# Six softmax multiplications moved from GpSimd to VectorE, and the start's small loads moved to other queues, in an attention and MLP kernel

## The chip, the cores and the metric

One Trainium2 chip, one core. The metric is the device time of one execution in microseconds (us). A ratio is the mean time of one kernel's runs over the mean time of the other's runs of the same rounds, so it is not quite the ratio of the medians that are quoted beside it.

Names in the profile: PE is the matrix engine and PEld its weight load; DVE is VectorE; ACT is ScalarE; POOL is GpSimd; SP issues most DMAs. A "q" behind an engine's name (ACTq) marks its instruction queue. L428 is line 428 of the kernel that was profiled. "n = 3" and the like are steps of the kernel's loop over pairs. A "half-clock window" is a stretch, some 3 us long or (after the longest stall) twice that in these traces, in which the granted clock is 0.50 and matrix instructions take about twice as long.

## The reference

```python
# q, k, v: (8, 12, 448, 64) float32; g_q, g_k: (64,); w_in: (768, 2048); w_out: (2048, 768)
def rmsnorm(x, g):
    rms = np.sqrt(np.mean(x * x, axis=-1, keepdims=True) + 1e-06)
    return x / rms * g
q_n, k_n = (rmsnorm(q, g_q), rmsnorm(k, g_k))
scores = scale * np.matmul(q_n, k_n.transpose(0, 1, 3, 2))
attn = np.exp(scores - max)                       # [cut: the maximum is taken off by row]
attn = attn / (np.sum(attn, axis=-1, keepdims=True) + 1e-09)
x = np.matmul(attn, v)                            # [cut: to (8*448, 12*64)]
h = x @ w_in
out = (h * (1.0 / (1.0 + np.exp(-h)))) @ w_out
```

## The kernel before

The kernel takes the heads two by two: 8 batches of 6 pairs, 48 pairs in all. The attention of a batch and the first matrix product of an earlier batch run interleaved, so PE always has something to do once the first batch is through. Only the first batch (pairs 0 to 5) has no product beside it, and there PE waits for the other engines.

The softmax is divided late: the exponentials are weighed with v, and the result x is multiplied by the reciprocal of the sums of the exponentials. The sums are made in two steps: DVE adds the chunks up (L428), then PE multiplies by ones (L444). DVE takes the reciprocal into `r[0]` (L448). For a couple of pairs six small DMAs spread it into `r[0]` and `r[1]`; a single pair (4 and 5 in the first batch) is divided at once.

```python
    def sums(members, width):
        t = ps.tile([P, S], F32, name="tr") if members[0] >= z.NPAIR else bank(S)
        for h in range(2):
            for i, n in enumerate(members):
                nc.tensor.matmul(                                            # L444
                    t[ds(h * D + i * width, width), :], ones[0:R, 0:width], es[n % 2][:, h, :],
                    start=True, stop=True,
                )
        nc.vector.reciprocal(out=r[0], in_=t)                                # L448

    def divide(n, t):
        engine = nc.gpsimd if n < z.NPAIR else nc.vector     # NPAIR is 6: the first batch
        x = xT(*pairs[n])
        engine.tensor_tensor(out=x, in0=x, in1=t, op=ALU.mult)               # L453
        state[n] = None

    def divide_by_sums(n):
        if n > 2 and n % 2 == 1 and not is_single(n - 2):
            for i in range(2):
                divide(n - 3 + i, r[i])              # n = 3: pairs 0, 1; n = 5: pairs 2, 3
        if n > 0 and is_single(n - 1):
            sums([n - 1], D)
            divide(n - 1, r[0])                      # n = 5: pair 4; n = 6: pair 5
        elif n > 0 and n % 2 == 0:
            sums([n - 2, n - 1], D // 2)             # n = 2: pairs 0, 1; n = 4: pairs 2, 3
            ...                                      # [cut: six small DMAs into r[0] and r[1]]
```

Rows are normalised by the same engines in turn: ACT squares, DVE sums the squares, POOL raises them to the power -1/2, and POOL multiplies q by that (for pair 0 DVE does).

```python
def normalise_rows(nc, z, rows, normal, squares, rms, minus_half, engine, together=True):
    for part in ([0, 1],) if together else ([0], [1]):
        for i in part:
            nc.scalar.activation(t, rows[name], AF.Square)                   # L297
            nc.vector.tensor_reduce(out=rms[:, i], in_=t, axis=AX.X, op=ALU.add)   # L298
        nc.vector.tensor_scalar(out=flat, in0=flat, ...)                     # L300
        nc.gpsimd.tensor_tensor(out=flat, in0=flat, in1=half, op=ALU.pow)    # L304
        if 0 in part:
            engine.tensor_tensor(out=by_head, in0=rows["q"], in1=factor, op=ALU.mult)  # L308
```

The start loads the rows of pairs 0 and 1, the gains `g_q` and `g_k` (as columns, for the factor of k), the same gains as rows (for a branch condition), and the first eight pieces of weights, 512 KB each. After the branch the rows of pair 2 are asked for.

```python
    load(state, 0)                                   # rows of pair 0, on SP
    for t, g in ((gq2, g_q), (gk2, g_k)):
        for half in range(2):
            nc.scalar.dma_start(t[ds(half * D, D), :], g.rearrange("(d one) -> d one", one=1))
    load(state, 1)
    for i, g in enumerate((g_q, g_k)):
        nc.sync.dma_start(g1[:, i, :], g.rearrange("(one d) -> one d", one=1))
    room = Room(nc, const, w_in, z)
    while room.w_in.load():                          # eight pieces of weights, 4 MB
        pass
    ...                                              # [cut: the condition on DVE, from g1]
    nc.vector.scalar_tensor_tensor(                                          # L258
        out=gains, in0=gq2, scalar=float(D) ** -0.5, in1=gk2, op0=ALU.mult, op1=ALU.mult
    )
    normalise_rows(...)                              # pair 0
    taken = nc.values_load(small[:1, :1], min_val=0, max_val=1)
    with tc.If(taken > 0) as cond:
        ...                                          # [cut]
    # in the branch:
    transpose(0, "k"); normalise(1); transpose(0, "q"); load(2, "qk")
    for n in range(last + 2):
        load(n + 3, "qk")
        scores(n, 0)
        weigh(n - 1, 1); load(n + 1, "v"); add_up(n - 1, 2, 3); unload(n - 1)
        transpose(n + 1, "q")
        ...                                          # [cut: divide_by_sums(n), second half]
```

Of the kernel before, what the change touches and what calls it, by code (L numbers as in the profile page):

```python
# [11 lines left out]
F32 = mybir.dt.float32  # L12
AF = mybir.ActivationFunctionType
ALU = mybir.AluOpType
# [154 lines left out]
@with_exitstack  # L169
def kernel(  # L170
    ctx: ExitStack,
    tc: tile.TileContext,
    q: bass.AP,
    k: bass.AP,
    v: bass.AP,
    g_q: bass.AP,
    g_k: bass.AP,
    w_in: bass.AP,
    w_out: bass.AP,
    out: bass.AP,  # L180
):











    nc = tc.nc
    z = Shapes(q, w_in)
    P, D, R, J = z.P, z.D, z.R, z.J

    const = ctx.enter_context(tc.tile_pool(name="const", bufs=1))

    n = 2 * J * D
    ring = const.tile([P, 7 * n], F32, name="rows")  # L200
    slots = [ring[0:R, ds(i * n, n)] for i in range(7)]
    rings = {"q": slots[0:2], "k": slots[2:5], "v": slots[5:7]}

    pairs = [(b, hp) for b in range(z.B) for hp in range(z.NPAIR)]
    state = [dict() for _ in pairs]

    sources = {"q": q, "k": k, "v": v}

    def load(state, n, names="qkv"):
        if n >= len(pairs):  # L210
            return
        b, hp = pairs[n]
        for name in names:

            order = "p j h d" if name == "k" else "p h j d"
            t = rings[name][n % len(rings[name])]
            t = t.rearrange(f"p ({order[2:]}) -> {order}", h=2, j=J)
            nc.sync.dma_start(
                t, sources[name][b, ts(hp, 2)].rearrange(f"h (p j) d -> {order}", j=J)
            )  # L220
            state[n][name] = t if name != "k" else t.rearrange("p j h d -> p h j d")


    load(state, 0)
    g1 = const.tile([1, 2, D], F32, name="g1")
    gq2 = const.tile([P, 1], F32, name="gq2")
    gk2 = const.tile([P, 1], F32, name="gk2")
    gains = const.tile([P, 1], F32, name="gains")
    for t, g in ((gq2, g_q), (gk2, g_k)):
        for half in range(2):  # L230
            nc.scalar.dma_start(t[ds(half * D, D), :], g.rearrange("(d one) -> d one", one=1))
    load(state, 1)
    for i, g in enumerate((g_q, g_k)):
        nc.sync.dma_start(g1[:, i, :], g.rearrange("(one d) -> one d", one=1))
    room = Room(nc, const, w_in, z)
    while room.w_in.load():
        pass
    ident = const.tile([P, P], F32, name="ident")
    make_identity(nc, ident)
    ones = const.tile([P, D], F32, name="ones")  # L240
    nc.gpsimd.memset(ones, 1.0)
    minus_half = const.tile([P, 1], F32, name="minus_half")
    nc.gpsimd.memset(minus_half, -0.5)
    first = const.tile([P, 1], F32, name="first")
    nc.scalar.activation(first, minus_half, AF.Square)

    small = const.tile([1, 1], I32, name="small")
    most = const.tile([1, 1], F32, name="most")
    both = const.tile([1, D], F32, name="both")
    nc.vector.tensor_tensor(out=both, in0=g1[:, 0, :], in1=g1[:, 1, :], op=ALU.mult)  # L250
    nc.vector.tensor_reduce(
        out=most, in_=both, axis=AX.X, op=ALU.max, apply_absolute_value=True
    )
    nc.vector.tensor_scalar(
        out=small, in0=most, scalar1=float(SCORE_MAX / D**0.5), scalar2=None, op0=ALU.is_le
    )

    nc.vector.scalar_tensor_tensor(  # L258
        out=gains, in0=gq2, scalar=float(D) ** -0.5, in1=gk2, op0=ALU.mult, op1=ALU.mult
    )  # L260


    normal = [const.tile([R, J, 2, D], F32, name=f"qn{i}") for i in range(2)]
    rms = [const.tile([R, 2, 2, J], F32, name=f"rms{i}") for i in range(4)]
    normalise_rows(
        nc, z, state[0], normal[0], normal[1].rearrange("p j h d -> p h j d"), rms[0], minus_half,
        nc.vector, together=False,
    )

    def arm():  # L270

        own = [dict(st) for st in state]
        r = copy.copy(room)
        r.w_in = copy.copy(room.w_in)
        return dict(
            tc=tc, nc=nc, z=z, pairs=pairs, state=own, load=lambda *a: load(own, *a), room=r,
            ring=ring, w_out=w_out, normal=(normal, rms), ident=ident, ones=ones, minus_half=minus_half, gains=gains,
            out=out,
        )

    taken = nc.values_load(small[:1, :1], min_val=0, max_val=1)
    with tc.If(taken > 0) as cond:
        with tc.manual_schedule():
            bounded(**arm())
    with cond.Else():
        general(**arm())


def normalise_rows(nc, z, rows, normal, squares, rms, minus_half, engine, together=True):


    by_head = normal.rearrange("p j h d -> p h j d")
    names = (("q", by_head), ("k", squares))
    for part in ([0, 1],) if together else ([0], [1]):
        for i in part:
            name, t = names[i]
            nc.scalar.activation(t, rows[name], AF.Square)  # L297
            nc.vector.tensor_reduce(out=rms[:, i], in_=t, axis=AX.X, op=ALU.add)  # L298
        flat = rms[:, ds(part[0], len(part))].rearrange("p i h j -> p (i h j)")
        nc.vector.tensor_scalar(  # L300
            out=flat, in0=flat, scalar1=1.0 / z.D, scalar2=1e-6, op0=ALU.mult, op1=ALU.add
        )
        half = minus_half[0 : z.R].to_broadcast([z.R, len(part) * 2 * z.J])
        nc.gpsimd.tensor_tensor(out=flat, in0=flat, in1=half, op=ALU.pow)  # L304
        if 0 in part:
            factor = rms[:, 0].rearrange("p h (j one) -> p h j one", one=1)
            factor = factor.to_broadcast([z.R, 2, z.J, z.D])
            engine.tensor_tensor(out=by_head, in0=rows["q"], in1=factor, op=ALU.mult)  # L308
# [16 lines left out]
def bounded(  # L325
# [4 lines left out]
    P, D, R, J, S = z.P, z.D, z.R, z.J, z.S  # L330
# [27 lines left out]
    normal, rms = normal  # L358
# [4 lines left out]
    def xT(b, c):  # L363
        return sets[b // 2 % 2].rearrange("p (b c s) -> p b c s", b=2, c=z.NW)[:, b % 2, c, :]
# [83 lines left out]
        nc.vector.reciprocal(out=r[0], in_=t)  # L448

    def divide(n, t):  # L450
        engine = nc.gpsimd if n < z.NPAIR else nc.vector
        x = xT(*pairs[n])
        engine.tensor_tensor(out=x, in0=x, in1=t, op=ALU.mult)  # L453
        state[n] = None

    def divide_by_sums(n):

        if n > 2 and n % 2 == 1 and not is_single(n - 2):
            for i in range(2):
                divide(n - 3 + i, r[i])  # L460
        if n > 0 and is_single(n - 1):
            sums([n - 1], D)
            divide(n - 1, r[0])
        elif n > 0 and n % 2 == 0:
            sums([n - 2, n - 1], D // 2)
            own = [t.rearrange("(h i p) s -> i h p s", h=2, i=2) for t in r]
            for i in range(2):
                for h in range(2):
                    nc.sync.dma_start(own[1][i, h], own[0][1, h])
            for h in range(2):  # L470
                nc.sync.dma_start(own[0][1, h], own[0][0, h])
# [621 lines left out]
```

## Time and profile before

| | before |
|---|---|
| median of 3 runs | 1469.49 us (1467.93 to 1470.61) |
| span of the profiled run | 1465.1 us |
| PE busy | 1432.2 us, 98% |
| where PE is not full | 0 to about 90 us, the start and the first batch |

The prediction below shows the page and the two stalls. A line of the timeline reads: start in us, busy us, engine, line, operation, output and inputs, their shapes, how many instructions in a row, and in brackets the idle time ahead of it and what ended that.

DVE's queue starts with a wait of 6.59 us for the gains, because the product of the gains stands first in it; the first copy of k (L390) comes at 13.05.

### The profile page before, as it was taken

What the parts mean: (1) busy time and instruction counts of PE and PEld (TensorE: products, weight loads), DVE (VectorE), ACT (ScalarE), POOL (GpSimd) and SP (SyncE); (2) the same over time, 40 slices, a digit from 0 to 9 for tenths busy, and PEclk for the clock granted to TensorE, in tenths of its full rate; (3) what the DMA queues carried; (4) which work ended last, traced back from release to release, by engine and by line L of the source; (5) the groups of instructions that cost most, each with busy time, mean ns of one, the idle gap of its engine ahead of it and who ended that gap; (6) DMA issues with size and microseconds to landing.
All of it is one profiled execution on the core that took longest, in us unless ns stands there. A gap on an engine that the chain in (4) does not pass through costs nothing.

```text
span 1465.1 us, 14059 instructions
## 1 busy us (share of the span) xinstructions
PE 1432.2 (98%) x5048; PEld 698.8 (48%) x5048; DVE 693.9 (47%) x915; ACT 568.7 (39%) x931; POOL 395.5 (27%) x250
## 2 busy tenths in 40 slices
PE   5989999999999999999999999999999999999998
PEld 2334444444444444444444445555555555555554
DVE  4777866656644545744544687722222222222220
ACT  6779886455555455455445344300000000000000
POOL 5765451333233333332332044410000000000000
PEclk9999999999999999999999999999999999999999
DMA  7524432222232223222221157422222222222220
GB/s 220 131 83 136 140 103 75 78 73 66 71 96 73 67 72 98 63 72 87 76 60 67 63 169 240 138 94 79 79 79 79 81 81 84 81 81 86 85 65 25
DMA packets 124660, 135.49 MB, mean 92 GB/s; under 512 B 50660, under 2 KB 106788, under 8 KB 124580
## 3 DMA queue, kind: packets, MB, share of 16 engines
q1 hardware_dynamic: 124260, 134.49, 30.2%
q8 instruction: 42, 0.69, 0.2%
q14 instruction: 38, 0.31, 0.1%
q10 hardware_dynamic: 320, 0.00, 0.0%
HBM read 87.56 MB, written 40.37 MB: 87 GB/s over the span
## 4 chain that ended last, share of the span: by engine, by line
PE 91%; DVE 4%; issue 1%; POOL 1%; ACT 1%; DMA 0%; ACTq 0%; DVEq 0%; POOLq 0%
PE mm L527 36%; PE sc L527 14%; PE sc L400 9%; PE av L416 9%; PE av L527 7%; PE tr L527 7%; PE mm L568 4%; PE tr L386 2%; PE tr L444 1%; PE tr L381 1%; DVE work L428 1%; DVE work L448 1%; DVE rms L298 1%; POOL rms L304 0%; DVE sums_x L475 0%
## 5 line engine op out<-in xcount | busy, mean ns | idle before, releaser
L405 ACT ACTIVATE work<-sc,rms 112x448 f32<-112x448 f32 x384 | 212.3, 636 | 177.7 <-PE sc L400 154.7
L304 POOL TENSOR_TENSOR rms<-rms,minus_half 112x16 f32<-112x16 f32 (+1 forms) x49 | 175.9, 3590 | 292.3 <-DVE rms L300 271.4
L527 PE MATMUL mm<-x,W 128*128 128x448 f32 x552 | 220.8, 541 | 0.7 <-ACT stage L534 0.6
L400 PE MATMUL sc<-work 64*112 64x448 f32 x768 | 173.2, 570 | 1.4 <-ACT work L390 0.7
L527 PE MATMUL mm<-sums_x,W 128*128 128x448 f32 x408 | 165.9, 542 | 0.7 <-DVE stage L478 0.5
L416 PE MATMUL av<-work,rows 112*64 112x448 f32 x768 | 165.7, 552 | 0.0
L428 DVE TENSOR_TENSOR work<-work 112x896 f32<-112x896 f32 x144 | 158.8, 1104 | 1.8
L527 PEld LDWEIGHTS mm<-x,W 128*128 128x128 f32 x552 | 101.8, 190 | 93.1 <-issue 88.0
L547 POOL TENSOR_TENSOR parts<-parts,stage 128x448 f32<-128x448 f32 (+1 forms) x33 | 37.2, 1128 | 314.2 <-DVE parts L478 302.7
L400 PEld LDWEIGHTS sc<-work 64*112 64x112 f32 x768 | 61.8, 175 | 104.5 <-issue 79.4
L527 PEld LDWEIGHTS mm<-sums_x,W 128*128 128x128 f32 x408 | 74.8, 190 | 68.9 <-issue 61.5
L448 DVE RECIPROCAL work<-tr 128x448 f32<-128x448 f32 x25 | 73.9, 2956 | 49.6 <-PE tr L444 49.6
L416 PEld LDWEIGHTS av<-work,rows 112*64 112x64 f32 x768 | 46.6, 136 | 105.9 <-issue 99.5
L547 POOL TENSOR_TENSOR parts<-parts,W 128x384 f32<-128x384 f32 x9 | 9.0, 995 | 307.8 <-DVE parts L478 307.8
L568 PE MATMUL mm<-x,W 128*128 128x448 f32 x192 | 75.9, 541 | 0.0
L534 ACT COPY stage<-mm 128x448 f32<-128x448 f32 (+1 forms) x30 | 15.7, 524 | 150.0 <-PE mm L527 144.0
L478 DVE TENSOR_TENSOR stage<-mm,parts 128x448 f32<-128x448 f32 (+1 forms) x51 | 31.4, 615 | 78.5 <-PE mm L527 51.6
L527 PE MATMUL mm<-W,work 128*128 128x384 f32 x204 | 68.6, 486 | 0.0
L392 DVE TENSOR_SCALAR work<-tr,gains 128x448 f32<-128x448 f32 x36 | 24.6, 684 | 89.3 <-PE tr L386 89.3
L653 ACT ACTIVATE stage<-stage 128x896 f32<-128x896 f32 x56 | 51.2, 945 | 36.8 <-DVE stage L478 35.9
L527 PE MATMUL sc<-W,work 128*128 128x384 f32 x192 | 64.5, 486 | 0.0
L298 DVE TENSOR_REDUCE rms<-qn 112x8 f32<-112x512 f32 x49 | 33.3, 681 | 55.7 <-ACT qn L297 53.5
(159 smaller groups left out, 1898.8 us busy)
## 6 DMA issues: line engine op xcount, KB each, us to landing
hidden<-stage SPq DMA_DIRECT2D x56, 448.0 KB, 2.8
work<-hidden SPq DMA_DIRECT2D x7, 2048.0 KB, 9.0
x<-hidden SPq DMA_DIRECT2D x7, 2048.0 KB, 8.9
W<-in_moe_w_in_dram SPq DMA_DIRECT2D x24, 512.0 KB, 4.1
rows<-in_moe_w_out_dram SPq DMA_DIRECT2D x32, 384.0 KB, 3.4
rows<-in_q_dram SPq DMA_DIRECT2D x48, 224.0 KB, 3.1
rows<-in_k_dram SPq DMA_DIRECT2D x48, 224.0 KB, 3.6
rows<-in_v_dram SPq DMA_DIRECT2D x48, 224.0 KB, 2.7
```

Source lines behind the costliest of these rows:

```text
L298: nc.vector.tensor_reduce(out=rms[:, i], in_=t, axis=AX.X, op=ALU.add)
L304: nc.gpsimd.tensor_tensor(out=flat, in0=flat, in1=half, op=ALU.pow)
L400: nc.tensor.matmul(banks[:, h, 0:S], kT[rows, ts(j, R)], qT[n % 2][rows, :], start=True, stop=True,)
L405: nc.scalar.activation(e[j][:, h, :], banks[:, h, 0:S], AF.Exp, scale=rms[n % 4][:, 1, h, j : j + 1])
L416: nc.tensor.matmul(st["av"][ds(h * D, D), :], st["v"][:, h, j, :], e[j][:, h, :], start=(j == 0), stop=(j == J - 1),)
L428: nc.vector.tensor_tensor(out=t, in0=e[0] if j == 1 else t, in1=e[j], op=ALU.add)
L448: nc.vector.reciprocal(out=r[0], in_=t)
L478: nc.vector.tensor_tensor(out=out, in0=a, in1=b, op=ALU.add)
L527: nc.tensor.matmul(t, self.left(name, s), self.right(name, s), start=s == ends[0], stop=s == ends[1])
L547: nc.gpsimd.tensor_tensor(out=u2, in0=u2, in1=p5, op=ALU.add)
L568: nc.tensor.matmul(h, room.w1(c, f), xT(b, c), start=(c == 0), stop=(c == z.NW - 1))
L653: nc.scalar.activation(t, t, AF.Silu)
```

## The change

There are two parts. All products by reciprocals go to DVE, to take POOL's queue out of DVE's way in the first batch. At the start the loads and the product of the gains and the loads for the condition change places among the queues, so that the branch and the first scores come earlier.

```diff
-    for t, g in ((gq2, g_q), (gk2, g_k)):
-        for half in range(2):
-            nc.scalar.dma_start(t[ds(half * D, D), :], g.rearrange("(d one) -> d one", one=1))
+    for i, g in enumerate((g_q, g_k)):
+        nc.scalar.dma_start(g1[:, i, :], g.rearrange("(one d) -> one d", one=1))
     load(state, 1)
-    for i, g in enumerate((g_q, g_k)):
-        nc.sync.dma_start(g1[:, i, :], g.rearrange("(one d) -> one d", one=1))
     room = Room(nc, const, w_in, z)
     while room.w_in.load():
         pass
+    minus_half = const.tile([P, 1], F32, name="minus_half")
+    nc.gpsimd.memset(minus_half, -0.5)
+    for t, g in ((gq2, g_q), (gk2, g_k)):
+        for half in range(2):
+            nc.gpsimd.dma_start(t[ds(half * D, D), :], g.rearrange("(d one) -> d one", one=1))
 [cut: minus_half was set further down]
-    nc.vector.scalar_tensor_tensor(
-        out=gains, in0=gq2, scalar=float(D) ** -0.5, in1=gk2, op0=ALU.mult, op1=ALU.mult
+    nc.gpsimd.tensor_tensor(out=gains, in0=gq2, in1=gk2, op=ALU.mult)
+    nc.gpsimd.tensor_scalar(
+        out=gains, in0=gains, scalar1=float(D) ** -0.5, scalar2=None, op0=ALU.mult
     )
 [cut]
     def divide(n, t):
-        engine = nc.gpsimd if n < z.NPAIR else nc.vector
         x = xT(*pairs[n])
-        engine.tensor_tensor(out=x, in0=x, in1=t, op=ALU.mult)
+        nc.vector.tensor_tensor(out=x, in0=x, in1=t, op=ALU.mult)
```

More of the change, by code (lines that the diff above doesn't have):

```diff
@@ L241 @@
     nc.gpsimd.memset(ones, 1.0)
-    minus_half = const.tile([P, 1], F32, name="minus_half")
-    nc.gpsimd.memset(minus_half, -0.5)
     first = const.tile([P, 1], F32, name="first")
@@ L276, in arm @@
             tc=tc, nc=nc, z=z, pairs=pairs, state=own, load=lambda *a: load(own, *a), room=r,
-            ring=ring, w_out=w_out, normal=(normal, rms), ident=ident, ones=ones, minus_half=minus_half, gains=gains,
-            out=out,
+            ring=ring, w_out=w_out, normal=(normal, rms), ident=ident, ones=ones,
+            minus_half=minus_half, gains=gains, out=out,
         )
```

## The prediction

> **What bounds the kernel now.** I first read the shares of busy time and the 40 slices of the page, to see where the matrix engine (PE) is not full.
>
> ```profile
> span 1465.1 us, 14059 instructions
> PE 1432.2 (98%) x5048; PEld 698.8 (48%) x5048; DVE 693.9 (47%) x915; ACT 568.7 (39%) x931; POOL 395.5 (27%) x250
> PE   5989999999999999999999999999999999999998
> ```
>
> PE is the bound: 1432.2 of 1465.1 us, so at most 33 us can be won by filling it, 2.2% of the span. The change only touches the first batch (pairs 0 to 5) and the start, where the digits 5, 9, 8 stand. So I read the busy time of each engine in stretches of 20 us.
>
> ```profile
> 50.00:70.00 20.00, 17.68 (x82) 6.02 (x82) 14.84 (x19) 14.94 (x28) 14.97 (x9) 0.91 0.56 142
> 70.00:90.00 20.00, 15.12 (x66) 5.62 (x67) 16.53 (x17) 11.83 (x22) 15.25 (x10) 0.83 0.20 59
> 90.00:110.00 20.00, 20.00 (x82) 8.22 (x81) 12.06 (x20) 17.28 (x30) 11.42 (x6) 1.00 0.36 111
> ```
>
> The columns are length, then busy time of PE, PE weight load, DVE, ACT, POOL, then granted clock. From 90 us on PE is full (20.00), so what is won before 90 us should stay won. Between 50 and 90 us PE lacks 2.3 and 4.9 us, and its clock fell to 0.91 and 0.83 on average. The timeline shows what it waited for, and the chain of waits behind that.
>
> ```profile
> 58.18 0.95 PE L444 MATMUL mm<-work,ones 112*32 112x448 f32 x6 [1.79 <-DVE work L428]
> 82.63 1.76 PE L444 MATMUL mm<-work,ones 112*64 112x448 f32 x4 [4.88 <-DVE work L428]
> 84.32 3.06 PE L400 MATMUL sc<-work 64*112 64x448 f32 x8
> ...
> 66.91 3.67 POOL L304 TENSOR_TENSOR rms<-rms,minus_half 112x16 f32<-112x16 f32 x1 [0.86 <-DVE rms L300]
> 70.65 1.04 POOL L308 TENSOR_TENSOR qn<-rows,rms 112x512 f32<-112x512 f32 x1
> 71.65 2.23 POOL L453 TENSOR_TENSOR x<-x,work 128x448 f32<-128x448 f32 x2
> 75.92 2.12 POOL L453 TENSOR_TENSOR x<-x,work 128x448 f32<-128x448 f32 x1 [2.04 <-ACT work L297]
> ...
> 72.82 2.96 DVE L448 RECIPROCAL work<-mm 128x448 f32<-128x448 f32 x1 [3.87 <-POOL x L453]
> 77.09 1.24 DVE L109 TENSOR_SCALAR W<-W 128x512 int32<-128x512 int32 x1
> ```
>
> PE lost 4.88 us because DVE's additions (L428) came late; they were late because the reciprocal (L448) overwrites r[0] and had to wait 3.87 us for POOL's multiplication that reads it; and that multiplication stood in POOL's queue behind a 3.67 us power and a 1.04 us product. PE's eight score instructions after the stall took 3.06 us, against 1.76 elsewhere in the same timeline.
>
> **What the Trainium skill says.** (1) "SBUF — State Buffer", section "Who interferes with whom": a VectorE instruction with two SBUF inputs, or in a two-port mode, and a GpSimd instruction that reads SBUF exclude each other, the second waiting until the first ends. The trace agrees for the big products: the one at 75.92 took 2.12 us beside L428 (ends 76.73), 1.14 otherwise; then L109 took 1.24 for its usual 0.43, ending 0.29 us after it. It does not for the power: three L428 at 46.91 took 3.21 us in all, about their usual 1.1 each, beside a power running from 47.08 to 50.97.
> (2) "TensorE: Matmul & The Clock Gate", Part 1: the clock is halved by windows of about 3.4 us with too little PE work. The trace agrees: in stretches of 2 us the granted clock is 0.50 at 60 to 62 and 82 to 86 us, after each of the two stalls.
> (3) "DMA: Bandwidth & Descriptors", Anatomy of one DMA: a DMA issued from GpSimd has about 2.0 us fixed cost. No such DMA is in this trace.
> (4) Same page, "Issuing engines are not separate DMA queues": another issuing engine saves only issue time. The start bears on this, below.
>
> **The change part by part.**
>
> *Multiplications of pairs 0 to 5.* POOL loses six, 8.8 us (6 x 1.466, the mean of the group). DVE gains six at 0.618 us (median of its own 42 in this line), 3.7 us. I took the instruction order of both built programs. For n = 3 the two now stand between add_up(2) and add_up(3); for n = 5 two stand ahead of the reciprocal and one after it; for n = 6 one after the reciprocal.
>
> n = 5: DVE's additions ahead end at 68.95. The reciprocals' copies: the earlier reciprocal ended at 62.23, six small DMAs took 4.4 us to issue (43.09 to 47.50) and 1.9 to land in the previous round, so about 68.5: no wait. Two products end at 70.2; reciprocal 70.2 to 73.15 instead of 72.82 to 75.78, 2.6 us earlier. Then +0.62 for the third product, and -0.81 since L109 no longer waits for POOL. The chain to PE's L444: 82.63 - 2.6 + 0.62 - 0.81, about 79.9; some contention of the freed POOL with L300 costs perhaps 0.15, so 80.05. **Direct gain 2.6 us.** PE's idle time shrinks from 4.88 to 2.3 us. Clock: before, the half clock lasted from about 80.2 to 87.0 with PE working 4.4 us of it, loss 2.2. If windows less than half busy trigger it (estimate from the two cases here), 2.3 us idle still triggers one window two times in three, loss 1.7, expected 1.15. **Clock gain about 1.0 us.**
>
> n = 3 and 4: the two products wait for the copies until about 49.6 (47.5 + 1.9 to 2.2), end at 50.9, so DVE is 0.8 us later than before; against that L300 at 55.01 took 1.00 us instead of 0.17 because POOL's L117 ran, pushed there by the products. POOL is 2.2 us earlier now, so L300 may be free, or L117 may fall on it again. **Gain 0 to 0.9, I take 0.5**, at the stall of 1.79 us. With 1.3 us idle the half clock (3.4 us, loss 1.7) would not come; it need not have come in every run before either. **Clock gain 1.0.**
>
> n = 6: the product leaves POOL (2.12 us at 87.61); nothing waited for it. 0.
>
> *Start.* ACT issues two DMAs less, so its table load begins near 2.0 instead of 3.32; DVE no longer waits until 6.59 for the gains; the condition is formed before the row products, not after 10.95. The branch can come 3 to 5 us earlier on PE. But POOL issues four DMAs and then waits for their landing before the two powers, so those start around 7 to 8.4 (estimate: four issues of 0.6 to 1 us as other queues' show, plus 2.9 to 3.7 us to landing as the same loads have now) against 8.18, and the gains are finished after them. The copy to kT moves from 13.05 to 10.6 to 12. But that meets another wall.
>
> ```profile
> rows<-in_k_dram SPq DMA_DIRECT2D x1, 224.0 KB, 8.8
> ...
> 21.61 0.62 ACT L297 ACTIVATE work<-rows 112x512 f32<-112x512 f32 x1
> ```
>
> The rows of pair 2, issued at 12.57, took 8.8 us to land, at 21.4: the weights' 4 MB are ahead of them, and the DMA engines are full from 4 to 19 us (share 0.94 to 1.28). ACT squares them at 21.61, ahead of the second half of pair 0's exponentials. Bytes and order are unchanged, so this landing moves by 0.3 us at most: of 1 to 3 us won, **0.3 to 0.5 remains**. PE, arriving earlier at the same wall, idles longer around 22 us and may be clocked down: about -0.4. Net 0.
>
> **Sum.** 2.6 + 1.0 + 0.5 + 1.0 + 0 = 5.1 us. 1469.5 - 5.1 = 1464.4; I say 1464.5.
>
> **Rivals.**
> A. *The start counts in full.* If the weights were not in the way (SP issues them about 0.8 us earlier), 3 us more are won: about 1461.5. For it: SP loses two issues and its waits. Against it: full DMA engines.
> B. *DVE becomes the bound of the first batch.* It is busy 16.5 of 20 us at 70 to 90 and gets 3.7 us more; products at n = 3 wait in its queue for copies, up to 1.2 us if these land as late as 3.2 us, and everything behind waits too. Then n = 4 is lost again and clock windows fall badly: about 1468.
> C. *POOL's new DMAs are slow.* If each holds POOL for over 1.5 us, powers start at 10 us or later and the start costs 1 to 2 us: about 1466.
> D. *PE goes to full clock in both places.* If neither stall reaches the threshold, another 1.2 us: about 1463, with A about 1460.
>
> **Range and chances.** The kernel before itself spans 2.7 us over three runs, likely by where the clock windows fall. A with D gives 1460, B 1468: range 1460.5 to 1468.0. Two per cent is 29 us; all PE idle time together is 33, so faster by over 2% has a chance of 0.005. Slower by over 2% would take a new wait in every pair: 0.005. Within 2%: 0.99.
>
> **What would show it.** PE's L444 stall near 80 us at 2 to 2.5 us, not 4.88, and DVE's reciprocal before it no longer waiting for POOL. At most one half-clock window there. ACT's first square of pair 2 now waiting for a DMA near 20.5 us, and the score instructions after it less than 1 us earlier than before: this right means the start is hidden. Product instructions on DVE near 0.62 us; over 1 would mean the port is contended. From 90 us on, PE full and the rest shifted by one constant. The prediction is wrong if PE stalls appear after 90 us that were not there, if the rows land 2 us earlier, or if POOL's DMA issues delay the powers beyond 9 us.

## More of the kernel before

In the changed kernel most lines of this study stand one further down (L428 becomes L429; the product stays L453).

The start of the kernel before, which the prediction only tells of, stands in its timeline of DVE, ACT and PE:

```profile
6.59 0.16 DVE L258 SCALAR_TENSOR_TENSOR gains<-gq,gk 128x1 f32<-128x1 f32 x1 [6.59 <-DMA gk<-in_g_k_dram]
13.05 0.63 ACT L390 ACTIVATE work<-tr,gains 128x448 f32<-128x448 f32 x1 [7.12 <-PE tr L386]
20.54 1.76 PE L400 MATMUL sc<-work 64*112 64x448 f32 x8
```

## The result, and the profile after

The changed kernel took 1464.11 us (median of 4 runs, 1462.75 to 1464.47) against 1469.79 us for the kernel before in the same rounds (4 runs, 1467.93 to 1470.61): ratio 0.9961, 95% interval 0.9944 to 0.9979, so 5.7 us or 0.4% less. The profiled spans, 1465.1 and 1462.3 us, differ by 2.8 us only. The profiled run of the kernel before, 1467.17 us, was quicker than all four of its timed runs; this matters below.

The page of the changed kernel: span, busy time, and PE's slices.

```profile
span 1462.3 us, 14057 instructions
PE 1431.8 (98%) x5048; PEld 698.9 (48%) x5048; DVE 696.1 (48%) x920; ACT 569.1 (39%) x931; POOL 389.9 (27%) x250
PE   5999999999999999999999999999999999999998
```

PE works as long as before (1431.8 for 1432.2 us); the third digit, the slice from 73 to 110 us, has gone from 8 to 9. DVE gained 2.2 us of busy time and POOL lost 5.6, less than the 3.7 and 8.8 of the six products, since other instructions of both became shorter or longer too. In the stretches of 20 us (length, then busy PE, PEld, DVE, ACT, POOL, then granted clock):

```profile
50.00:70.00 20.00, 17.41 (x92) 6.15 (x88) 18.23 (x24) 16.46 (x32) 13.99 (x7) 1.00 0.60 151
70.00:90.00 20.00, 17.94 (x78) 6.85 (x76) 18.24 (x23) 13.97 (x26) 10.55 (x7) 0.91 0.31 83
```

Between 70 and 90 us PE is busy 17.94 us where it was 15.12, and its clock is 0.91 where it was 0.83. Between 50 and 70 us the clock is full, 1.00 for 0.91: PE is "busy" less there (17.41 for 17.68) although it got through more instructions (92 for 82), because at full speed each is shorter. The timeline after, of PE at the three sums, and of DVE and POOL ahead of them:

```profile
59.32 0.95 PE L445 MATMUL mm<-work,ones 112*32 112x448 f32 x6 [1.19 <-DVE work L429]
69.45 0.97 PE L445 MATMUL mm<-work,ones 112*64 112x448 f32 x4 [1.41 <-DVE work L429]
80.26 1.64 PE L445 MATMUL mm<-work,ones 112*64 112x448 f32 x4 [2.06 <-DVE work L429]
...
52.55 1.61 POOL L309 TENSOR_TENSOR qn<-rows,rms 112x512 f32<-112x512 f32 x1
...
69.31 1.15 DVE L453 TENSOR_TENSOR x<-x,work 128x448 f32<-128x448 f32 x2
70.47 2.96 DVE L449 RECIPROCAL work<-mm 128x448 f32<-128x448 f32 x1
73.53 0.62 DVE L453 TENSOR_TENSOR x<-x,work 128x448 f32<-128x448 f32 x1
```

The stall of 4.88 us is 2.06 us, the one of 1.79 us is 1.19. The reciprocal starts at 70.47 right behind the two products, with no wait for POOL; the products take 0.58 and 0.62 us on DVE.

The start, in the timelines of POOL, ACT and PE:

```profile
8.35 0.19 POOL L258 TENSOR_TENSOR gains<-gq,gk 128x1 f32<-128x1 f32 x1 [4.12 <-DMA gk<-in_g_k_dram]
8.49 3.27 POOL L305 TENSOR_TENSOR rms<-rms,minus_half 112x8 f32<-112x8 f32 x2
12.07 0.63 ACT L391 ACTIVATE work<-tr,gains 128x448 f32<-128x448 f32 x1 [5.09 <-POOL gains L259]
22.19 0.63 ACT L298 ACTIVATE qn<-rows 112x512 f32<-112x512 f32 x1 [1.55 <-DMA rows<-in_q_dram]
23.31 0.63 ACT L298 ACTIVATE work<-rows 112x512 f32<-112x512 f32 x1 [0.49 <-DMA rows<-in_k_dram]
26.61 1.76 PE L401 MATMUL sc<-work 64*112 64x448 f32 x8 [1.49 <-ACT work L391]
```

The view of DMA issues between 11 and 14 us has these rows take 10.2 us to land, where it was 8.8 before:

```profile
rows<-in_k_dram SPq DMA_DIRECT2D x1, 224.0 KB, 10.2
```

The copy of k is 1.0 us earlier than before (12.07 for 13.05). Then ACT waits for the rows of pair 2, which landed near 22.2 and 23.3 us, and the scores of pair 1 begin at 26.61, where the kernel before had 24.90. So in this pair of profiles the start **lost** 1.7 us. Both luck and the change are in this. Six profiles have the old start with all eight weights ahead (before, e1, e5, e9, e10, e11): in two the scores of pair 1 begin at 24.90 and 25.14 us, in four, where PE ran the batch ahead of them at half clock, at 26.72 to 27.09. That is the luck. That the rows land later belongs to the change; see "The start" below.

### The profile page after: what moved, and what is told of

It is laid out like the page before. It is cut to its first block, busy times and chain, and to the rows that moved or that the text cites. A ratio compares the mean times of both kernels' runs of the same rounds, so it can differ in the third digit from the quotient of the medians. Undisturbed runs are those within 1.5% of the kernel's fastest.

```text
span 1462.3 us, 14057 instructions
## 1 busy us (share of the span) xinstructions
PE 1431.8 (98%) x5048; PEld 698.9 (48%) x5048; DVE 696.1 (48%) x920; ACT 569.1 (39%) x931; POOL 389.9 (27%) x250
## 4 chain that ended last, share of the span: by engine, by line
PE 91%; DVE 4%; DMA 2%; ACT 2%; issue 1%; SPq 0%; POOL 0%; DVEq 0%; ACTq 0%; POOLq 0%
PE mm L527 36%; PE sc L527 13%; PE sc L401 10%; PE av L417 9%; PE av L527 7%; PE tr L527 7%; PE mm L568 4%; PE tr L387 2%; PE tr L445 1%; PE tr L382 1%; DVE work L429 1%; DMA rows<-in_k_dram 1%; DVE work L449 1%; DVE rms L299 0%; DMA W<-in_moe_w_in_dram 0%
## 5 line engine op out<-in xcount | busy, mean ns | idle before, releaser
L429 DVE TENSOR_TENSOR work<-work 112x896 f32<-112x896 f32 x144 | 159.0, 1105 | 1.8
```

The costliest lines, as they stand in the source:

```text
L429: nc.vector.tensor_tensor(out=t, in0=e[0] if j == 1 else t, in1=e[j], op=ALU.add)
```

## The experiments

Theory: the whole gain comes from the products, through DVE's chain to the sums and through PE's clock; the start is worth nothing, because the weights' transfers, which stand ahead of the rows of pair 2, delay these rows (called the wall below). Rivals: the start gives part of the gain, or takes part of it away (its four loads from POOL are slow); the gain is the freed tile `r[0]` alone and not the engine; the clock matters little.

All results, each against the kernel before in the same rounds (9 runs of it in each of three groups, medians 1469.54, 1469.81 and 1469.63 us):

| run | what it is | median us | ratio | 95% interval |
|---|---|---|---|---|
| e1_products | before, products on DVE | 1464.13 | 0.9960 | 0.9947 to 0.9974 |
| e2_start | before, start changed | 1469.20 | 0.9996 | 0.9983 to 1.0010 |
| e3_gains_act | changed, gains loaded from ACT | 1463.88 | 0.9955 | 0.9942 to 0.9969 |
| e4_late_w | changed, half of the weights later | 1461.22 | 0.9936 | 0.9922 to 0.9949 |
| e5_own_r | before, own reciprocals for pairs 4, 5 | 1467.45 | 0.9983 | 0.9970 to 0.9997 |
| e6_no_gains | changed, no loads of gains (wrong result) | 1464.22 | 0.9957 | 0.9942 to 0.9973 |
| e7_products_late_w | e1 and half of the weights later | 1463.39 | 0.9953 | 0.9939 to 0.9966 |
| e9_fill | before, 3 and 9 useless products on PE | 1468.74 | 0.9991 | 0.9978 to 1.0005 |
| e10_fill5 | before, 1 and 5 useless products on PE | 1466.53 | 0.9984 | 0.9970 to 0.9997 |
| e11_first_two | before, products of pairs 0, 1 on DVE | 1468.85 | 0.9994 | 0.9980 to 1.0008 |
| e12_late_w_again | e4 once more | 1460.94 | 0.9942 | 0.9928 to 0.9955 |
| e8_gains_last | e4, gains' product behind the powers | 1459.86 | 0.9932 | 0.9918 to 0.9945 |

### e1: the products alone

```diff
-        engine = nc.gpsimd if n < z.NPAIR else nc.vector
-        engine.tensor_tensor(out=x, in0=x, in1=t, op=ALU.mult)
+        nc.vector.tensor_tensor(out=x, in0=x, in1=t, op=ALU.mult)
```

> The kernel before with the multiplications of pairs 0 to 5 on VectorE and nothing else changed. Theory 1 (products are the gain, the new start is a loss of about 1.7 us, as the two profiles stand at the first score products of pair 1: 24.90 us before, 26.61 changed): about 4.5 us less than before plus what before loses to a second clock window in its slower runs, so 1.5 to 2 us faster than the whole change; PE stalls near 56 and near 79 us of 1.2 and 2.1 us at the same lengths as in the changed kernel, reciprocal no longer waiting for POOL. Theory 2 (the late start was chance of one run, the start is neutral): the same time as the whole change within 0.5 us.

It took 1464.13 us, the time of the whole change, as theory 2 expects. Its stalls at the three sums, 0.97, 1.42 and 2.06 us, are those of the whole change within 0.22 us. PE's timeline:

```profile
21.35 3.33 PE L400 MATMUL sc<-work 64*112 64x448 f32 x8
27.09 1.76 PE L400 MATMUL sc<-work 64*112 64x448 f32 x8
...
79.92 1.76 PE L444 MATMUL mm<-work,ones 112*64 112x448 f32 x4 [2.06 <-DVE work L428]
```

Its start is the code of the kernel before, yet the second batch of scores took 3.33 us from 21.35, not 1.76 from 20.54. The start of unchanged code thus differs by more than a microsecond from run to run, with where the half-clock stretch falls (scores of pair 1 at 27.09 us here, 24.90 in the profile of before).

### e2: the start alone

```diff
 [the diff of the change without its last part]
```

> The changed kernel with the multiplications back on GpSimd: only the start is new. Theory 1: 1 to 2 us slower than before; first score products of pair 1 near 26.6 us, rows of pair 2 landing 1.5 to 2 us later than before (22.2 and 23.3 us). Theory 2: within 0.5 us of before, those score products near 24.9 us. Both: the reciprocal again waits 3 to 4 us for POOL's product.

It took 1469.20 us: ratio 0.9996, so the start is worth 0.6 us, give or take 2. The timeline of PE's last sums, and of ACT at the rows of pair 2:

```profile
83.64 1.76 PE L445 MATMUL mm<-work,ones 112*64 112x448 f32 x4 [4.89 <-DVE work L429]
...
22.28 0.63 ACT L298 ACTIVATE qn<-rows 112x512 f32<-112x512 f32 x1 [1.43 <-DMA rows<-in_q_dram]
```

The stall of 4.89 us is whole again, and the rows of pair 2 come as late as in the changed kernel, behind a wait for the DMA. Since this run has the changed kernel's start, and its scores of pair 1 begin at 26.63 for 26.61 us, the two profiles may be compared step by step without the luck of the start. That is done under "Why the prediction was right" below.

### e3: the gains loaded from ACT

```diff
-            nc.gpsimd.dma_start(t[ds(half * D, D), :], ...)
+            nc.scalar.dma_start(t[ds(half * D, D), :], ...)
```

> The changed kernel with the four loads of the gains issued on ScalarE's queue instead of GpSimd's, all else as changed. Theory A (the loads through GpSimd's queue are what slows the row transfers at the start: 110 to 248 GB/s between 3 and 7 us, against 156 to 279): the rows of pair 0 (k) land by about 5.3 us instead of 6.3, those of pair 2 near 20.7 and 21.4, score products of pair 1 by 24.9 us or earlier, and the whole is 1.5 to 2 us faster than the change. Theory B (something else, as the earlier issue of the rows or of the condition's loads, slows them): pair 2 still lands at 22 to 23 us and the time is that of the change.

The copy of k came at 11.19 us, 0.9 earlier than in the changed kernel, but ACT then waited 2.98 us for the rows of pair 2 (to 22.73 us), and the scores of pair 1 began at 27.09. The time, 1463.88 us, cannot be told from 1464.11. What is won ahead of the rows is waited away at the rows.

### e4 and e12: half of the weights later

```diff
-    while room.w_in.load():
-        pass
+    for _ in range(4):
+        room.w_in.load()
 [cut: in the branch]
     load(2, "qk")
+    while room.w_in.load():
+        pass
```

> The changed kernel with only four of the eight early weight transfers issued ahead of the branch, the other four after the rows of pair 2. Theory (the rows of pair 2, behind 4 MB of weights, are the wall that hides what the start wins, as predicted): rows of pair 2 land by about 16 to 18 us, ScalarE's first square of pair 2 no longer waits for a DMA, score products of pair 1 start near 23 us instead of 26.6, and the whole is 2.5 to 3.5 us faster than the change. Rival (the chain behind is bound elsewhere, by POOL's power or the clock): less than 1 us.

With 2 MB instead of 4 MB ahead of them the rows of pair 2 land after 6.3 and 7.1 us. In the view of DMA issues between 10 and 14 us (bytes and us from issue to landing), and in ACT's timeline, which now has no wait there:

```profile
rows<-in_q_dram SPq DMA_DIRECT2D x1, 224.0 KB, 6.3
rows<-in_k_dram SPq DMA_DIRECT2D x1, 224.0 KB, 7.1
...
20.85 0.63 ACT L298 ACTIVATE qn<-rows 112x512 f32<-112x512 f32 x1
```

The scores of pair 1 began at 25.77 us, not near the 23 expected: the batch ahead of them ran at half clock (3.33 us from 20.32). The kernel took 1461.22 us, ratio 0.9936. A second time, in another group:

> The kernel of e4 once more, so that e8 has it on the same chip and in the same rounds: ratio to before 0.9936 again, within 0.001, if the first result was not luck.

This time 1460.94 us, ratio 0.9942. By the two ratios it is 8.5 to 9.4 us faster than before, and about 3 us faster than the changed kernel (0.9961). So with the changed start the weights ahead of the rows do cost time. But less than half of the 3 us is the wall itself: PE's last sums of the first batch come 1.3 us earlier than in the changed kernel (78.91 and 78.99 for 80.26), and the scores after the next product 3.0 and 2.9 us earlier (86.72 and 86.79 for 89.70), because neither e4 nor e12 had a half-clock window at n = 6. This does not look like the luck of two profiles alone: the mean granted clock was 0.999 in eight of the ten timed runs of e4 and e12, and 0.998 in all four of the changed kernel. Why late weights spare the window is not shown.

### e7: half of the weights later, with the old start

```diff
 [the edits of e1 and of e4 in the kernel before]
```

> The kernel before with the products on VectorE and four of the eight weight transfers late, with the start of before otherwise. Theory (the wall of the weights hides the new start, so with the wall gone the new start shows): 1 to 1.5 us slower than the changed kernel with late weights (1461.2), near 1462.5. Rival (the new start is worth nothing with or without the wall): the same as that one within 0.5 us, and all of its gain is from the late weights.

It took 1463.39 us, ratio 0.9953: late weights alone give 1.0 us over e1 (0.9960), which is within the noise of two intervals of 0.0027. Against e4 and e12 (0.9936 and 0.9942) it is 1.6 to 2.5 us slower. So the changed start is worth about 2 us, but only where the rows do not wait behind the weights. The intervals of e7 and e4 overlap, so this size is an estimate from three ratios; in the profiles PE's last sums come 0.9 us earlier (78.91 and 78.99 for 79.84). Nor did late weights bring those sums forward with the old start (79.84 for 79.92 in e1): there ACT never waited for the rows of pair 2.

### e6: no loads of gains at all

```diff
-    for t, g in ((gq2, g_q), (gk2, g_k)):
-        for half in range(2):
-            nc.gpsimd.dma_start(t[ds(half * D, D), :], ...)
+    for t in (gq2, gk2):
+        nc.gpsimd.memset(t, 1.0)
```

> Wrong result on purpose: the changed kernel with gq2 and gk2 set to 1 by memset instead of the four loads through GpSimd. Theory A (these loads slow the row transfers at the start): rows of pair 2 land by 21 us, score products of pair 1 near 25 us, DMA rate between 4 and 6 us back near 250 GB/s from 197. Theory B (the loads are innocent, the order of the others is not): still 22 us and 197 GB/s. The time falls by 1 to 2 us under A, by under 0.5 us under B.

Its output is wrong, which doesn't matter for the time. It takes away all that the gains can cost: PE's first scores began at 10.00 us instead of 14.39. The timeline of ACT, then PE, at the rows of pair 2:

```profile
21.51 0.63 ACT L297 ACTIVATE qn<-rows 112x512 f32<-112x512 f32 x1 [5.66 <-DMA rows<-in_q_dram]
...
26.03 3.33 PE L400 MATMUL sc<-work 64*112 64x448 f32 x8 [6.87 <-ACT work L390]
```

ACT waited 5.66 us for the same rows, PE stood 6.87 us and then ran its eight scores at half clock, 3.33 us. Four microseconds won at 10 us were worth nothing: 1464.22 us. Neither theory came true whole: the transfer rate at 4 to 6 us rose to 279 GB/s as theory A has it, the time did not fall. This is the strongest evidence that what is won ahead of these rows is lost at them.

### e8: the product of the gains behind the powers

```diff
 [on top of e4: the two gpsimd instructions on gains stand after normalise_rows of pair 0]
```

> The changed kernel with four of the eight early weight transfers after the rows of pair 2 (as e4), and the two products of the gains behind POOL's two powers instead of ahead of them, so that the powers no longer wait for the gains' landing. With the wall of weights gone, theory 'the gains' landing now sets the start' expects the copies to kT 1.0 to 2.5 us earlier than in e4 and the whole kernel 1 to 2 us faster than e4 of the same call (ratio to before about 0.9925). Rival 'the rows of pair 1 or 2, or PE's own work, bind already': within 0.7 us of e4.

POOL no longer waits for the gains ahead of its powers. In the timelines of POOL and ACT:

```profile
7.88 2.02 POOL L305 TENSOR_TENSOR rms<-rms,minus_half 112x8 f32<-112x8 f32 x1 [1.19 <-DVE rms L301]
9.87 0.18 POOL L266 TENSOR_TENSOR gains<-gq,gk 128x1 f32<-128x1 f32 x1
10.47 0.63 ACT L391 ACTIVATE work<-tr,gains 128x448 f32<-128x448 f32 x1 [3.59 <-POOL gains L267]
```

The copy of k comes at 10.47 us, 1.6 us earlier than in e12 (12.09), and PE's last sums of the first batch 1.3 us earlier (77.67 for 78.99). The time is 1459.86 us against 1460.94 in the same rounds, ratios 0.9932 and 0.9942. The intervals overlap, so the timed gain of 1.0 to 1.5 us is likely but not shown; that the chain is shorter is shown by the trace. The profiled run was the slowest of its five (1461.71 us) and had a half-clock window at n = 6 that e12's had not. This is the best version, 10 us below the kernel before, and its result is correct.

### e11: only pairs 0 and 1 on DVE

```diff
-        engine = nc.gpsimd if n < z.NPAIR else nc.vector
+        engine = nc.gpsimd if 2 <= n < z.NPAIR else nc.vector
```

> The kernel before with only the products of pairs 0 and 1 (n = 3) on DVE; those of pairs 2 to 5 stay on POOL. The prediction put 0.5 us direct and 1.0 us of clock at this place, of 5.1 in all: its theory expects 1 to 2 us faster than before (ratio about 0.999), the stall at n = 4 near 1.0 to 1.2 us and the one at n = 6 still near 4.9. Rival 'nearly all of the gain comes from n = 5 and 6': within 0.5 us of before.

PE's timeline has the first stall shortened and the last one whole:

```profile
57.85 0.95 PE L444 MATMUL mm<-work,ones 112*32 112x448 f32 x6 [1.23 <-DVE work L428]
81.62 1.76 PE L444 MATMUL mm<-work,ones 112*64 112x448 f32 x4 [4.88 <-DVE work L428]
```

The gain was 0.9 us by the ratio, with an interval from 2.9 us faster to 1.2 us slower. That is just below the 1 to 2 us expected, and neither they nor the rival (nearly nothing) are ruled out. What it does show is that about half of the 5.7 us, or more, is not at this place.

### e5: own tiles for the reciprocals of pairs 4 and 5

```diff
-        nc.vector.reciprocal(out=r[0], in_=t)
+        own = parts[:, ts(members[0] % 2, S)] if len(members) == 1 and members[0] < z.NPAIR else r[0]
+        nc.vector.reciprocal(out=own, in_=t)
+        return own
 [cut: divide(n - 1, own)]
```

> The kernel before, multiplications still on GpSimd, but the reciprocals of pairs 4 and 5 go to tiles of their own instead of r[0]. Theory 1 (the wait for r[0] is what the change removes): the reciprocal near 70 us starts without a wait for POOL, the PE stall near 80 us falls from 4.9 to about 2 us, and the time is 3 to 4.5 us below before (all of the n = 5 gain, without the extra product on VectorE, not the n = 3 gain). Theory 2 (GpSimd's share of the SBUF port and its late products are the cause, the tile is not): less than 1 us, since POOL's products still block L109 for 0.8 us and still come late.

The products stay on POOL, but the reciprocal need not wait for them. The timeline of DVE, then POOL:

```profile
70.81 2.96 DVE L449 RECIPROCAL parts<-mm 128x448 f32<-128x448 f32 x1 [1.07 <-PE mm L444]
73.69 3.04 DVE L428 TENSOR_TENSOR work<-work 112x896 f32<-112x896 f32 x1
...
72.44 2.23 POOL L455 TENSOR_TENSOR x<-x,work 128x448 f32<-128x448 f32 x2
74.62 1.15 POOL L455 TENSOR_TENSOR x<-x,parts 128x448 f32<-128x448 f32 x1
```

The wait of 3.87 us for POOL is gone: the reciprocal now waits 1.07 us, for PE. But the next addition, usually 1.03 us, took 3.04 us: it reads two tiles while POOL's three products read theirs, and ended 0.96 us after the last of these. PE's stall was 3.29 us instead of 4.88 and the gain 2.5 us by the ratio (0.4 to 4.4), less than half of what moving the products gives. Theory 1 expected a stall of about 2 us and 3 to 4.5 us in time, theory 2 less than 1 us; neither holds alone. So the tile is about 1.6 of the 2.8 us of that stall, and what the tile gives back is partly taken again by the shared port (point 1 of what the prediction quotes). Moving the products to DVE removes both.

### e9 and e10: useless work for PE in the stalls

```diff
     def sums(members, width):
+        idle = {2: 3, 5: 9}.get(members[0], 0) if members[0] < z.NPAIR else 0   # e10: {2: 1, 5: 5}
+        for _ in range(idle):
+            nc.tensor.matmul(t[0:D, :], ones, room.chunk(0)[:, 0:S], start=True, stop=True)
```

The result stays right, since the sums overwrite the bank. Nothing is made faster by this but the clock.

> The kernel before with useless matrix products in the two PE stalls (3 ahead of the sums at n = 4, 9 at n = 6, each about 0.44 us), overwritten at once, nothing else changed. Theory (stalls halve PE's clock for a window of 3.4 us, and that costs extra): no half-clock stretch between 55 and 90 us, stalls of the same length or shorter, time 1.5 to 3 us below before. Rival (the clock stretches cost nothing since PE waits anyway): within 0.5 us of before.

The clock stayed full, but I had mis-sized the filling. One useless product took 0.73 us and not 0.44, so the nine took 6.6 us, and the last sums came about 1.5 us after DVE was ready for them. Time 1468.74 us, ratio 0.9991: inconclusive. Sized anew:

> The kernel before with useless products on PE in its two stalls, one at n = 4 and five at n = 6, now sized with the 0.73 us that each took in e9, so 0.73 and 3.65 us against stalls of 1.79 and 4.88 us: PE is not late for its sums any more, only kept at work. Theory 'about half of the loss at the stalls is the halved clock after them': no half-clock stretch between 55 and 90 us, the eight scores after the sums 1.76 us instead of 3.06, and the kernel 1.5 to 3 us faster than before (ratio 0.998 to 0.999). Rival 'the clock falls elsewhere anyway, or matters little': within 0.7 us of before.

PE's timeline, the five useless products (two records each) and what follows:

```profile
78.50 3.97 PE L444 MATMUL mm<-W,ones 128*64 128x448 f32 x10
83.45 0.97 PE L449 MATMUL mm<-work,ones 112*64 112x448 f32 x4 [0.98 <-DVE work L428]
84.36 1.76 PE L400 MATMUL sc<-work 64*112 64x448 f32 x8
```

The eight scores after the sums took 1.76 us instead of 3.06, no stretch between 54 and 88 us had less than full clock, and the kernel took 1466.53 us: ratio 0.9984, 2.4 us faster than before, with an interval from 0.4 to 4.4 us. Useful work did not change and no wait went away. So in the kernel before the clock after the stalls costs about 2.4 us, with that interval.

## Why the prediction was right

The time was 1464.11 for 1464.5, inside the range. That the sum came so near is partly luck: 1.0 us for the clock at n = 4 was too much, and the other four steps brought about 1.1 us more than predicted. The steps, each by what carried it:

| step | predicted us | measured us | from |
|---|---|---|---|
| n = 3 and 4, direct | 0.5 | 0.6 | sums at 59.93 in e2, 59.32 in the changed kernel |
| n = 5 and 6, direct | 2.6 | 2.8 | the last stall, 4.89 to 2.06 |
| clock after n = 6 | 1.0 | 1.2 | what PE gains after the sums, 90.70 to 86.15 less 3.4 |
| clock after n = 4 | 1.0 | 0 here, 1.6 in the profile of before | see below |
| start | 0 | 0.6, give or take 2 | e2 |
| whole change | 5.1 | 5.7 | the timed ratio; e1 alone 5.9 |

The middle column compares e2, which has the changed start and the old products, with the changed kernel, which has both. Their first scores of pair 1 lie 0.02 us apart. Along PE the sums of n = 4 then come 0.61 us earlier and those of n = 6 come 3.38 us earlier. The next transposes of k, after the half-clock stretch, start at 90.70 and 86.15, 4.55 us apart, and from there the distance stays at 4.55. The three steps thus make 4.6 us in these profiles, whose spans differ by 4.8; by the timed ratios (0.9996 and 0.9961) it is 5.1.

**The chain through `r[0]`.** This was right: the reciprocal stopped waiting for POOL, and the last stall is 2.06 us (predicted 2.3). The third product on DVE did cost 0.62 us. e5 adds what the prediction had not separated: without the tile's wait, POOL's products would still have blocked DVE's addition.

**The clock at n = 6.** Right in kind and size. e10 shows the loss without touching anything else. As foreseen, not every run is alike: a stall of 2.06 or 2.07 us gave one half-clock window in the profiles of the changed kernel, e1, e6 and e8, and none in those of e3, e4, e7 and e12. That is four of eight, where the prediction said two in three for 2.3 us.

**The clock at n = 4.** This step was too sure. The profiled run of before had a half-clock window there, and e2, with a stall of 1.77 us for 1.79, and e5, with 1.79 as well, had none from 58 to 68 us. So it goes with the run and not with the length of the stall alone. Nor is it lost in full where it comes: in the profile of before PE, late from the half clock, waited only 0.53 us at the sums of n = 5, and where it was not late it waited 1.41 in the changed kernel. DVE sets that point. My estimate from these profiles is that the prediction's 1.0 us should have been a few tenths on the mean of runs; e11's 0.9 us for direct gain and clock together agrees but does not settle it.

**The port at n = 3.** The prediction left open whether POOL would fall on DVE again there. It did, in another place: POOL's product of q (L309) ran 1.61 us from 52.55, beside an addition (L429, to 52.91) and L109 on DVE, and L109 took 1.15 us from 53.29, where 0.43 is usual. This cost nothing in the profile, since DVE then waited 0.38 us for ACT. The gain of 0.6 is the one that the prediction had hoped for: L301, slowed beside POOL's L117 to 0.96 us in e2, took 0.18, and ACT's square ahead of it came 0.16 us later.

**The start.** "Net 0" was right in the time, and that what comes earlier waits for the rows of pair 2 is shown by e3 and e6, and by e4 from the other side. The step that failed is "this landing moves by 0.3 us at most". With the old start and all weights ahead the rows of k landed at 21.3 to 22.0 us in six profiles (issue plus time to landing), and ACT never waited for them; with the changed start they landed at 23.2 us in two (the changed kernel and e2), and ACT waited. So the prediction took for fixed a wall that did not bind the kernel before and that the change moved back by more than 1 us. That the net is still near 0 is luck of the clock: with the old start PE began the scores of pair 1 at 26.72 to 27.09 us in four of six profiles, because the batch ahead ran at half clock; with the changed start they begin at 26.61 and 26.63, even where that batch ran at full clock (e2). In stretches of 2 us the transfers moved 155 and 197 GB/s at 2 to 4 and 4 to 6 us, against 174 and 250 before. Without the loads of gains (e6) the rate at 4 to 6 us was 279, and yet the rows were squared at 21.51 and 22.73 at the earliest. So the gains' loads seem to slow the early transfers (one profile without them), but that is not the whole of the later landing; the rest stays open.

**Rival A** (the start counts in full) did not occur, and e4 and e8 show what it would have taken; the 0.8 us by which SP should have issued the weights earlier was 0.09 (5.58 for 5.67). **Rival B** (DVE the bound) was half there: DVE is busy 18.2 of 20 us in both stretches, 91%, and all three stalls that remain are waits for L429. **Rival C** (POOL's DMAs too slow) was right in kind and small: issuing took 2.4 us for four, the gains were waited for until 8.35, the powers began at 8.49 (9.10 in e2), and e8 shows 1.6 us of it on the chain. **Rival D** came true in the profiles of e3, e4, e7 and e12, not in that of the changed kernel.

**The luck of a profile.** The two profiles differ by 2.8 us where the medians differ by 5.7. The kernel before was profiled in a run with a warm PE at 20.54 us; e1, with the same code there, ran cold. A difference of one pair of profiles has this much chance in it, and only a third run that shares one part with each (e2) made the sum by steps come out.

## What to carry to other kernels

When a wait is put down to a tile that another engine still reads, look at what stands ahead of that reader in its queue, and count both costs: the wait for the tile and the slower instructions on a shared port. A stall of the matrix engine can cost more than its length, because the clock may stay halved after it (about 2.4 us for two stalls here, e10); a cheap test is to fill the stall with useless products, sized from a measured duration. And a gain ahead of a late transfer can be worth nothing (e6) until the transfer's place in the queue is moved, so try both together.

## What the Trainium skill lacked or had wrong

- "TensorE: Matmul & The Clock Gate", Part 1, says that the windows run free, which fits that the same stall halves the clock in one run and not in another. It puts the half clock after at least one idle window of about 3.4 us; here shorter stalls did it too: 1.79 us in the profile of before and not in e5, 2.06 us in four profiles of seven; 4.88 us did in every profile read unless filled (e9, e10). It lacks what such a loss is worth when the sums behind it wait for another engine anyway.
- "SBUF — State Buffer", "Who interferes with whom", says that a VectorE instruction with two SBUF inputs and a GpSimd instruction that reads SBUF exclude each other. That holds for products (e5: 3.04 us instead of 1.03). It did not hold for GpSimd's power of 112x16 elements: three additions on DVE beside one took 3.21 us, their usual time, and the power 3.89 us for its usual 3.67.
- "DMA: Bandwidth & Descriptors", Anatomy of one DMA, gives about 2.0 us fixed for a DMA issued from GpSimd. Here the four loads of 256 bytes each took 3.8 and 4.9 us (median of each two) to land in the changed kernel, beside full-size transfers, and the same loads from ACT's queue took 2.9 and 3.7 us in the kernel before and 3.7 and 3.7 us in e3, where only the queue differs. The page gives no figure for a DMA that shares the engines with others.
- No page that I read gives a figure for how far a few loads of one 4-byte element for each partition slow the large transfers beside them. Here the rate at 4 to 6 us was 178 to 197 GB/s with them from POOL (five profiles), 217 with them from ACT (e3) and 279 without them (e6, one profile). With the old start, where they were issued first, it was 221 to 252 in seven profiles, so their place may count too.
